# One beat's delay for the weight preparation that falls on the first beat of a softmax chunk

## The chip, the cores and the metric

The kernel runs on one core of a Trainium2 chip. The metric is the time of one execution in microseconds (us), as the median of several runs. The engines are TensorE (PE in the profile, with its weight loads as PEld), VectorE (DVE), ScalarE (ACT), GpSimd (POOL) and SyncE (SP, which here only issues DMAs). They run side by side, each in its own program order, and wait for each other by semaphores.

## The reference

Attention with normalised queries and keys over 8 batches of 12 heads, 448 rows and 64 columns, and behind it a feed-forward block with a maximum of three products. All is float32.

```
q_n, k_n = rmsnorm(q, g_q), rmsnorm(k, g_k)
scores = scale * q_n @ k_n^T
attn = softmax(scores)                       # row maximum subtracted
attn_out = attn @ v                          # (8, 12, 448, 64)
x = attn_out as (3584, 768)
h = maximum(maximum(x @ w1, x @ w2), x @ w3) # (3584, 768)
out = h @ w_out                              # (3584, 768)
```

## The kernel before

Two heads make a pair; there are 48 pairs `g`, six to a batch. The 448 rows of a pair are worked in four chunks `c` of 112 rows. The program is a list of beats: `beat(g, i)` with `i` from 0 to 11, three beats to a chunk, so the beat's number is `12 g + i` and the first beat of a chunk is one whose number is divisible by 3. Every engine's order is the order in which the beats issue its instructions; nothing reorders them afterwards.

For a chunk numbered `k = 4 g + c` the steps are:

- first beat: `row_max` (L562, DVE) finds the negated maxima of the two heads' scores; `softmax` scales them (`nm`, L570, ACT) and takes two exponentials with their row sums (L579, ACT); then `lower_weights` of the chunk before (L665, DVE, two instructions) runs, the last reader of that chunk's scores.
- second beat: `upper_weights` takes the reciprocal of the sums (`rs`, L648 and L652, DVE) and writes the softmax weights as float16 (`pp`, L655, ACT, two instructions).
- third beat: PE does the scores of the next chunk (L553). The scores live in two PSUM buffers in turn, so they need the buffer that `lower_weights` of the chunk before has read.

Each number is kept as an upper float16 part and a lower one (the rest), and three products of parts make one product. The first six pairs (`PLAIN = 6`) are done otherwise, in plain float32.

Beside that, `thirds` issues in each beat two or three steps of the feed-forward block of an earlier batch (L732 layer 1, L796 layer 2), which fill PE. Further work is put off with `later(beats, work, last)` into the table `due`; `tick`, the last call of a beat, issues what is due at the current number `clock[0]`, first the works without `last`, then those with it.

The weights are prepared in 24 blocks: 18 of w1, w2 and w3, then 6 of w_out. In the program's view they come as pairs of 32-bit words. `prep_block(n)` is called at the first beat after `4 n` for n up to 18 and at the first after `72 + 8 (n - 18)` beyond. It has these steps:

- `rebias` (L188, ACT), at once;
- `decode` in three stages 2, 3 and 4 beats later (L196, L200, L205, DVE);
- for a block of w_out `row_largest` (L170, DVE) 5 beats later, and `load_raw` (L223 or L228, SP), the load of block n + 2 into the one of two buffers that the decode has emptied.

After the third block of a column group, `bound_in` takes its maximum and turns it into a scale, and then each of the three blocks is split: `upper` (L268, L269, ACT) and two beats later `lower` (L272, POOL). After the last block `bound_out` does the same for w_out, where `upper` (L307, ACT) and `lower` (L312, DVE) of the six blocks follow at one beat's distance. The unsplit block lies one slot on from where its split parts go, so `upper` of a block overwrites what `lower` of the block before reads.

Of the kernel before, what the change touches and what calls it, by code (L numbers as in the profile page):

```python
# [35 lines left out]
PLAIN = 6  # L36
# [3 lines left out]
def qknorm_attention_maxout_ffn_kernel(  # L40
# [69 lines left out]
    due = {}  # L110
    clock = [0]

    def later(beats, work, last=False):

        due.setdefault(clock[0] + beats, ([], []))[last].append(work)

    def tick():
        while clock[0] in due:
            for works in due.pop(clock[0]):
                for work in works:  # L120
                    work()
        clock[0] += 1


    ident = const.tile([P, P], F32, name="ident")
# [51 lines left out]
    o_row = const.tile([P, NFT], F32, name="o_row")  # L177
# [56 lines left out]
    def prep_block(n):  # L234
        kind, ft, j = blocks[n]
        raw = raws[n]
        f = plain(w_sb, n) if kind == "in" else plain(wo_sb, ft)
        rebias(raw)

        for stage in range(3):  # L240
            later(2 + stage, lambda stage=stage: decode(raw, f, stage), True)
        if kind == "out":
            later(5, lambda: row_largest(o_row[:, ft:ft + 1], f), True)
        later(5, load_raw)
        if j == NJ - 1:
            later(5, lambda: bound_in(ft), True)
        elif kind == "out" and ft == NFT - 1:
            later(6, bound_out)

    def bound_in(ft):  # L250
        most = sb.tile([P, 1], F32, name="most", bufs=2)
        n = ft * NJ + 1
        row_largest(
            most, w_sb[:, n:n + NJ].rearrange("p n a f -> p (n a f)").bitcast(F32)
        )

        def scale(bound):
            top, up = w_most[:, ft:ft + 1], w_up[:, ft:ft + 1]
            nc.vector.tensor_scalar(
                out=top, in0=bound, scalar1=LEAST, scalar2=None, op0=ALU.max  # L260
            )
            nc.vector.reciprocal(up, top)
            nc.vector.tensor_scalar(
                out=up, in0=up, scalar1=UP, scalar2=None, op0=ALU.mult
            )

            def upper(n, f):
                nc.scalar.activation(f, f, AF.Copy, scale=up)  # L268
                nc.scalar.copy(w_sb[:, n, 0], f)  # L269

            def lower(n, f):
                nc.gpsimd.tensor_tensor(  # L272
                    out=w_sb[:, n, 1], in0=f, in1=w_sb[:, n, 0], op=ALU.subtract
                )

            for j in range(NJ):
                n = ft * NJ + j
                f = plain(w_sb, n)
                later(2 + 4 * j, lambda n=n, f=f: upper(n, f), True)
                later(4 + 4 * j, lambda n=n, f=f: lower(n, f), True)  # L280

        largest(most, scale, (3, 2, 4, 1))


    def bound_out():
        by = const.tile([P, NFT], F32, name="o_block")
        most = const.tile([P, 1], F32, name="o_most")
        nc.vector.tensor_tensor(out=by, in0=o_row, in1=w_most, op=ALU.mult)
        nc.vector.tensor_reduce(most, by, axis=AX, op=ALU.max)

        def scale(bound):
            nc.vector.tensor_scalar(
                out=o_up, in0=bound, scalar1=LEAST ** 2, scalar2=None, op0=ALU.max
            )
            nc.vector.reciprocal(most, o_up)
            nc.vector.tensor_scalar(
                out=by, in0=w_most, scalar1=most, scalar2=2.0 * UP,
                op0=ALU.mult, op1=ALU.mult,
            )

            nc.vector.tensor_scalar(
                out=o_up, in0=o_up, scalar1=DM / 2.0 / (2.0 * UP), scalar2=None,
                op0=ALU.mult,
            )

            def upper(ft):
                nc.scalar.activation(  # L307
                    wo_sb[:, ft, 0], plain(wo_sb, ft), AF.Copy, scale=by[:, ft:ft + 1]
                )

            def lower(ft):
                nc.vector.scalar_tensor_tensor(  # L312
                    out=wo_sb[:, ft, 1], in0=plain(wo_sb, ft), scalar=by[:, ft:ft + 1],
                    in1=wo_sb[:, ft, 0], op0=ALU.mult, op1=ALU.subtract,
                )
                split.append(ft)

            for ft in range(NFT):
                later(ft + 1, lambda ft=ft: upper(ft), True)
                later(ft + 2, lambda ft=ft: lower(ft), True)  # L320

        largest(most, scale, (1, 2, 2, 2))


# [600 lines left out]
    def beat(g, i):  # L925
        w, n = g - 1, g + 2
        c, part = divmod(i, 3)
        k = 4 * g + c
        early = k + 1 <= 4 * PLAIN
        if part == 0:  # L930
            if g < G:
                if k > 4 * PLAIN:
                    row_max(g, c)
                softmax(g, c)
            if early:
                scores(*divmod(k + 1, 4))
            if 0 < k <= 4 * PLAIN:
                turn_plain(*divmod(k - 1, 4))
            elif 0 < k <= 4 * G:
                lower_weights(*divmod(k - 1, 4))  # L940
        if part == 1:
            if 0 < k <= 4 * PLAIN:
                keep_turned(*divmod(k - 1, 4))
            if PLAIN <= g < G:
                upper_weights(g, c)
        if part == 2:
            if early:
                row_max(*divmod(k + 1, 4))
            elif k + 1 < 4 * G:
                scores(*divmod(k + 1, 4))  # L950
        if 0 <= w < PLAIN:
            if i == 1:
                guard_sums(w)
            if i == 2:
                inverse_sums(w)
            if i == 5:
                spread_sums(w)
            if i == 6:
                keep_sums(w)
            if i == (8 if w < PLAIN else 9):  # L960
                scale_plain(w)
        if w >= 0 and i == (4 if w < PLAIN else 7):
            add_values(w)
        thirds(THIRDS[i] + (len(queue) > 1 and i % 6 == 4))
        if w >= 0 and i == (9 if w < PLAIN else 10):
            finish(w, x_of[w // NP])
        if w >= 0 and g % NP == 0 and i == (6 if w < PLAIN else 10):
            queue.append(ffn(w // NP, x_of[w // NP]))

        if g + 1 < G:  # L970
            if g + 1 < PLAIN:
                if i in (1, 4):
                    turn_whole(g + 1, "kq"[i // 4])
                if i in (2, 5):
                    keep_whole(g + 1, "kq"[i // 5])
            else:
                if i in (0, 1):
                    upper_rows(g + 1, "kq"[i])
                if i in (2, 3):
                    lower_rows(g + 1, "kq"[i - 2])  # L980
                if i in (4, 5):
                    turn_rows(g + 1, "kq"[i - 4])

        if n < G:
            if i in (0, 3):
                squares(n, "kq"[i // 3])
            if i in (2, 5):
                sum_squares(n, "kq"[i // 3])
            if i in (5, 7):
                inv_rms(n, "kq"[i // 7])  # L990
            if i == 8:
                scale_k(n)
            if i == 9:
                scale_q(n)

        if g == 0 and i < 7:
            load_v(i)
            later(3, lambda: largest_v(i))
        if 0 < g < G - 6 and i == 5:
            load_v(g + 6)  # L1000
            later(4, lambda: largest_v(g + 6))
        if g == 0 and i == 9:
            bound_v(0)
        if g > 1 and g % NP == 0 and g < G and i == 1:
            bound_v(g // NP)
        if PLAIN <= g < G and i == 9:
            scale_v(g)
        if PLAIN <= g < G and i == 11:
            upper_v(g)
        if PLAIN <= w and i == 0:  # L1010
            lower_v(w)

        if g + 3 < G:
            if i == 0:
                load_k(g + 3)
            if i == 1:
                load_q(g + 3)
        if i == 2 and w >= PLAIN:
            turn_weights(w, 3)
        if PLAIN <= g < G and i in (5, 8, 11):  # L1020
            turn_weights(g, i // 3 - 1)
        n_in = min(decoded[0], NFT * NJ)
        due_at = BLOCK_BEATS[0] * n_in + BLOCK_BEATS[1] * (decoded[0] - n_in)
        if decoded[0] < len(blocks) and clock[0] > due_at:
            later(0, lambda n=decoded[0]: prep_block(n), True)
            decoded[0] += 1
        tick()

# [40 lines left out]
```

## Time and profile before

| | |
|---|---|
| median of 3 runs | 1101.73 us |
| lowest, highest | 1098.24, 1102.97 us |
| the profiled execution | 1103.44 us |
| its span, first to last instruction | 1101.6 us |
| mean granted TensorE clock | 0.957 |
| busy: PE, DVE, ACT, POOL | 1018.6, 757.8, 772.1, 702.4 us |

In the rows of the profile the first two numbers of an instruction are its start in us from the beginning of the span and its duration; then come engine, line, operation, the tile written and those read, their shapes, and how many were merged (x2). Square brackets hold the idle time of the engine just before, and whose work ended it. A row of waits names who waited, for whom, the total, the number of times and the longest. A row of groups gives the busy time and the mean duration in ns. Granted clock 1.00 is full speed.

### The profile page before, as it was taken

How to read it: one execution, taken by the hardware profiler on the slowest of the kernel's cores; microseconds unless marked ns; L12 is line 12 of the kernel's file. 1: busy time of each engine (PE TensorE's matmuls, PEld its weight loads, DVE VectorE, ACT ScalarE, POOL GpSimd, SP SyncE). 2: the span in 40 equal slices, each digit the busy share in tenths (PEclk: the TensorE clock that was granted, in tenths of full speed). 3: DMA queues.
4: the chain of work that ended last, by engine and by line, in shares of the span. 5: the costliest groups of instructions: out<-in, count | busy, mean ns of one | idle time of the engine just before them, and what ended most of it. 6: DMA issues, size and time to landing. Idle time of an engine off the chain costs nothing. (4 is left out here: it accounts for less than half of the span.)

```text
span 1101.6 us, 18390 instructions
## 1 busy us (share of the span) xinstructions
PE 1018.6 (92%) x6168; PEld 501.9 (46%) x6168; DVE 757.8 (69%) x1390; ACT 772.1 (70%) x1767; POOL 702.4 (64%) x805
## 2 busy tenths in 40 slices
PE   4678768988999999999999999999999999999998
PEld 2334333434444455444544454444444454445555
DVE  3899988888667676677677776777677766762210
ACT  4599887767868678687877777778777787773001
POOL 5477988856767767678677686776867677610000
PEclk9687868998989999999999999999999999999999
DMA  5554466856787679877888789787877798563002
GB/s 149 165 164 152 129 180 137 179 115 125 151 166 149 134 151 172 160 148 133 176 155 149 136 169 175 141 151 150 170 146 143 145 166 153 106 106 73 1 1 58
DMA packets 426654, 152.29 MB, mean 138 GB/s; under 512 B 372928, under 2 KB 422336, under 8 KB 426560
## 3 DMA queue, kind: packets, MB, share of 16 engines
q1 hardware_dynamic: 425888, 150.75, 66.8%
q8 instruction: 48, 0.79, 0.3%
q10 hardware_dynamic: 672, 0.38, 0.1%
q14 instruction: 46, 0.38, 0.1%
HBM read 51.97 MB, written 11.01 MB: 57 GB/s over the span
## 5 line engine op out<-in xcount | busy, mean ns | idle before, releaser
L732 PE MATMUL acc<-xt,w_sb 128*128 128x448 f16 x2592 | 520.6, 356 | 0.6 <-ACT m L742 0.6
L732 PEld LDWEIGHTS <-w_sb 128*128 128x128 f16 x2592 | 245.1, 99 | 262.9 <-issue 53.1
L562 DVE TENSOR_REDUCE sc<-sc 112x2 f32<-112x896 f32 x192 | 209.7, 1092 | 47.8 <-PE sc L553 46.6
L579 ACT ACTIVATE sc<-sc,nm,down 112x448 f32<-112x448 f32 x336 | 234.2, 697 | 11.2
L655 ACT ACTIVATE pp<-sc,rs 112x448 f16<-112x448 f32 x336 | 194.8, 632 | 48.5 <-ACT sc L579 40.4
L665 DVE SCALAR_TENSOR_TENSOR pp<-sc,rs,pp 112x448 f16<-112x448 f32 x336 | 212.9, 675 | 3.4 <-ACT pp L655 2.9
L387 POOL TENSOR_TENSOR ri<-ri,half_neg 128x7 f32<-128x7 f32 x96 | 154.2, 1606 | 8.0
L553 PE MATMUL sc<-kt,qt 64*112 64x448 f16 x1008 | 133.7, 371 | 27.1 <-DVE pp L665 23.6
L570 ACT ACTIVATE nm<-sc,down 112x2 f32<-112x2 f32 x192 | 50.7, 264 | 149.5 <-DVE sc L562 148.2
L796 PE MATMUL acc<-wo_sb,ht 128*128 128x384 f16 x864 | 151.4, 330 | 1.4 <-DVE ht L756 0.8
L761 POOL COPY hx<-ht 128x128 f16<-128x128 f16 x48 | 15.5, 323 | 197.7 <-DVE ht L756 191.7
L796 PEld LDWEIGHTS <-ht 128*128 128x128 f16 x864 | 82.0, 99 | 67.5 <-issue 14.5
L703 PE MATMUL av<-pt,vp 128*64 128x448 f16 x1008 | 108.3, 356 | 0.0
L553 PEld LDWEIGHTS <-qt 64*112 64x112 f16 x1008 | 55.0, 128 | 96.9 <-issue 56.4
L648 DVE TENSOR_SCALAR rs<-sc 112x2 f32<-112x2 f32 x168 | 26.6, 158 | 94.7 <-ACT sc L579 94.7
L440 POOL TENSOR_TENSOR kp<-kn,kp 128x512 f16<-128x512 f32 x42 | 50.0, 1190 | 58.9 <-ACT kp L434 58.9
L703 PEld LDWEIGHTS <-vp 128*64 128x64 f16 x1008 | 49.6, 108 | 56.0 <-issue 30.4
L718 DVE SCALAR_TENSOR_TENSOR xt<-av,xt 128x448 f16<-128x448 f32 x42 | 26.2, 625 | 71.1 <-ACT xt L717 71.1
L372 DVE TENSOR_REDUCE ss<-sq 128x7 f32<-128x448 f32 x96 | 60.9, 635 | 10.6 <-ACT sq L363 6.6
L531 POOL TENSOR_TENSOR vp<-vr,vp 128x448 f16<-128x448 f32 x42 | 43.8, 1044 | 32.2 <-ACT vp L525 32.1
L440 POOL TENSOR_TENSOR qp<-qn,qp 112x512 f16<-112x512 f32 x42 | 49.3, 1173 | 21.0 <-ACT qp L434 20.8
L517 POOL TENSOR_SCALAR vr<-vr,v_up 128x448 f32<-128x448 f32 x42 | 60.7, 1446 | 0.0
(112 smaller groups left out, 1203.1 us busy)
## 6 DMA issues: line engine op xcount, KB each, us to landing
raw<-in_moe_w_dram SPq DMA_DIRECT2D x18, 768.0 KB, 4.4
qr<-in_q_dram SPq DMA_DIRECT2D x48, 224.0 KB, 3.0
vr<-in_v_dram SPq DMA_DIRECT2D x96, 96.0 KB, 2.5
kr<-in_k_dram SPq DMA_DIRECT2D x95, 96.0 KB, 3.0
raw<-in_moe_w_out_dram SPq DMA_DIRECT2D x6, 768.0 KB, 5.1
pt<-pp SPq DMA_TRANSPOSE x168, 4.1
out_dram<-osb SPq DMA_DIRECT2D x8, 336.0 KB, 3.2
out_dram<-osb SPq DMA_DIRECT2D x8, 288.0 KB, 3.7
```

What stands on the lines that cost most here:

```text
L372: nc.vector.tensor_reduce(sums[g % 2][:sq.shape[0], KQ[what]], sq, axis=AX, op=ALU.add)
L387: nc.gpsimd.tensor_tensor(out=ri, in0=ri, in1=half_neg[:, at], op=ALU.pow)
L440: nc.gpsimd.tensor_tensor(out=parts[:, 1], in0=n, in1=parts[:, 0], op=ALU.subtract)
L517: nc.gpsimd.tensor_scalar(out=vr, in0=vr, scalar1=v_up[:, g // NP:g // NP + 1], scalar2=None, op0=ALU.mult,)
L553: nc.tensor.matmul(sc[:QP, h, :S], qt[rows, qp, c], kt[rows, kp, KEYS[h]], start=n == 0, stop=n == len(TERMS) - 1,)
L562: nc.vector.tensor_reduce(sc[:QP, 0, S + 8:S + 10], sc[:QP, :, :S], axis=AX, op=ALU.max, negate=True)
L579: nc.scalar.activation(to, sc[:QP, h, :S], AF.Exp, bias=nm[:, h:h + 1], scale=down[:QP], accum_out=total,)
L655: nc.scalar.activation(pp[:, 0, h], sc[:QP, h, :S], AF.Copy, scale=rs[:, h:h + 1])
L665: nc.vector.scalar_tensor_tensor(out=pp[:, 1, h], in0=sc[:QP, h, :S], scalar=rs[:, h:h + 1], in1=pp[:, 0, h], op0=ALU.mult, op1=ALU.subtract,)
L703: nc.tensor.matmul(av[half, :S], vp[rows, group, vpart], pt[rows, 7 * wp + group], start=u == 0 and n == 0, stop=u == 3 and n == len(TERMS ...
L732: nc.tensor.matmul(acc[:, :S], wt[:, wp, c], xs[c][:, xp], start=(c == 0 and n == 0), stop=(c == NCT - 1 and n == 2),)
L796: nc.tensor.matmul(acc[:, :HW], lhs, wo_sb[:, f, wp, half * HW:(half + 1) * HW], start=(f == 0 and n == 0), stop=(f == NFT - 1 and n == 2),)
```

## The change

`later` gets a fourth argument that names an engine. When `tick` comes to a work with such a name in a beat whose number is divisible by 3 and at least `12 * PLAIN = 72`, which is the first beat of a chunk from the seventh pair on, it does not issue the work but puts it at the head of the `last` list of the next beat. Named are the decode stages, the maxima and the loads, `prep_block` itself and the split of the weights, but for `lower` of w1 to w3 on POOL. `load_raw` and `bound_out` also move from the first list to the `last` one. `prep_block` counts its later steps from the beat in which it is issued, so a block whose preparation is put off has all its steps one beat later. No instruction is added, removed or altered.

```
-    def later(beats, work, last=False):
+    def later(beats, work, last=False, on=None):
-        due.setdefault(clock[0] + beats, ([], []))[last].append(work)
+        due.setdefault(clock[0] + beats, ([], []))[last].append((work, on))
+
+    def busy(on):
+        return on is not None and clock[0] % 3 == 0 and clock[0] >= 12 * PLAIN

     def tick():
+        put_off = []
         while clock[0] in due:
             for works in due.pop(clock[0]):
-                for work in works:
-                    work()
+                for work, on in works:
+                    if busy(on):
+                        put_off.append((work, on))
+                    else:
+                        work()
         clock[0] += 1
+        if put_off:
+            due.setdefault(clock[0], ([], []))[1][:0] = put_off
...
         for stage in range(3):
-            later(2 + stage, lambda stage=stage: decode(raw, f, stage), True)
+            later(2 + stage, lambda stage=stage: decode(raw, f, stage), True, "dve")
         if kind == "out":
-            later(5, lambda: row_largest(o_row[:, ft:ft + 1], f), True)
-        later(5, load_raw)
+            later(5, lambda: row_largest(o_row[:, ft:ft + 1], f), True, "dve")
+        later(5, load_raw, True, "dve")
         if j == NJ - 1:
-            later(5, lambda: bound_in(ft), True)
+            later(5, lambda: bound_in(ft), True, "dve")
         elif kind == "out" and ft == NFT - 1:
-            later(6, bound_out)
+            later(6, bound_out, True, "dve")
...
-                later(2 + 4 * j, lambda n=n, f=f: upper(n, f), True)
+                later(2 + 4 * j, lambda n=n, f=f: upper(n, f), True, "act")
                 later(4 + 4 * j, lambda n=n, f=f: lower(n, f), True)
...
-                later(ft + 1, lambda ft=ft: upper(ft), True)
-                later(ft + 2, lambda ft=ft: lower(ft), True)
+                later(ft + 1, lambda ft=ft: upper(ft), True, "act")
+                later(ft + 2, lambda ft=ft: lower(ft), True, "dve")
...
-            later(0, lambda n=decoded[0]: prep_block(n), True)
+            later(0, lambda n=decoded[0]: prep_block(n), True, "act")
```

## The prediction

> **What bounds the kernel now.** I read the page, then the stretches in time, then the waits and instructions of the one stretch that the change reaches.
>
> ```profile
> span 1101.6 us, 18390 instructions
> ...
> PE 1018.6 (92%) x6168; PEld 501.9 (46%) x6168; DVE 757.8 (69%) x1390; ACT 772.1 (70%) x1767; POOL 702.4 (64%) x805
> ...
> raw<-in_moe_w_out_dram SPq DMA_DIRECT2D x6, 768.0 KB, 5.1
> ```
>
> ```profile
> 140.00:285.00 145.00, 122.52 (x683) 58.05 (x684) 122.23 (x213) 110.65 (x238) 111.01 (x113) 0.87 0.67 145
> 285.00:1000.00 715.00, 703.15 (x4441) 342.34 (x4439) 508.44 (x1001) 543.21 (x1273) 494.29 (x590) 1.00 0.78 149
> ```
>
> The columns of the second view are the stretch, then busy time of PE, weight loads, DVE, ACT, POOL, then granted clock. TensorE bounds the whole. From 285 us on it is busy 98% (703.15 of 715) at clock 1.00, so only a gap or a slow clock before that can be gained or lost. The moved work is all issued between beats 72 and 133 (a beat is `12 g + i`), about 145 to 273 us by their rows below. There PE is busy 84%, as is DVE, and the clock is 0.87: neither engine bounds it alone, but the chain between them.
>
> ```profile
> ACT nm L570 <- DVE sc L562: 21.5, 13, 3.0
> PE sc L553 <- DVE pp L665: 16.3, 8, 3.9
> ...
> DVE rs L648 <- ACT sc L579: 9.5, 13, 1.4
> ```
>
> These are waits in the same 145 us (total, times, longest). PE's scores of chunk k+2 wait for `lower_weights(k)` (L665) on DVE, which frees the score buffer: 16.3 us over 8 waits, the most that better DVE order could give back besides the clock. L665 stands on DVE behind the `row_max` (L562) of chunk k+1. The last row is what matters here: after `lower_weights` of the chunk before, DVE mostly waits for ScalarE's exponentials before `rs` (L648). That gap is in the chunk's first beat, where the moved DVE work stood. After `rs` DVE goes on to the next `row_max` mostly without a gap.
>
> ```profile
> 175.32 2.44 PE L732 MATMUL acc<-xt,w_sb 128*128 128x448 f16 x12
> ...
> 182.08 1.37 PE L553 MATMUL sc<-kt,qt 64*112 64x448 f16 x6 [2.41 <-DVE pp L665]
> 183.38 4.63 PE L732 MATMUL acc<-xt,w_sb 128*128 128x448 f16 x12
> ...
> 211.19 0.78 PE L553 MATMUL sc<-kt,qt 64*112 64x448 f16 x6 [1.02 <-DVE pp L665]
> ...
> 222.48 0.78 PE L553 MATMUL sc<-kt,qt 64*112 64x448 f16 x6 [1.66 <-DVE pp L665]
> ...
> 229.26 1.37 PE L553 MATMUL sc<-kt,qt 64*112 64x448 f16 x6 [2.49 <-DVE pp L665]
> ...
> 270.64 1.37 PE L553 MATMUL sc<-kt,qt 64*112 64x448 f16 x6 [3.22 <-DVE pp L665]
> ```
>
> A PE wait has a second price. After 1.66 us idle the scores took 0.78, after 2.41 and more 1.37, and 12 matmuls then took 4.63 where 2.44 is usual: a slow restart costs (1.37 - 0.78) + (4.63 - 2.44) = 2.8 us.
>
> **The change part by part.** A block n from 18 on is prepared at beat 73 + 8(n - 18), decoded 2, 3 and 4 beats later, its maximum and the next load 5 later. Work tagged `dve` or `act` and due at a beat divisible by 3, from 72, goes one later: stage 1 of block 17 (72), stage 0 of 18 (75), maximum of 18, load, `upper` of 13 (78), rebias of 19 (81, and with it all its stages, of which those that land on 84 and 87 move twice), `upper` of 16 (90), stage 2 of 20 (93), stage 0 of 21 (99), its maximum and load (102), rebias of 22 (105, its stages likewise), stage 2 of 23 (117), and of w_out `upper` 2 and `lower` 1 (129), `upper` 5 and `lower` 4 (132). No instruction is added or removed.
>
> ```profile
> 145.18 1.35 DVE L200 SCALAR_TENSOR_TENSOR w_sb<-raw,w_sb 128x768 uint32<-128x768 uint32 x1
> 147.93 0.16 DVE L648 TENSOR_SCALAR rs<-sc 112x2 f32<-112x2 f32 x1 [1.41 <-ACT sc L579]
> ...
> 148.26 2.68 DVE L205 SCALAR_TENSOR_TENSOR w_sb<-raw,w_sb 128x768 uint32<-128x768 uint32 x1
> ...
> 156.11 0.55 DVE L196 TENSOR_SCALAR wo_sb<-raw 128x768 uint32<-128x768 uint32 x1
> 156.92 0.16 DVE L648 TENSOR_SCALAR rs<-sc 112x2 f32<-112x2 f32 x1 [0.27 <-ACT sc L579]
> ...
> 161.96 0.94 DVE L170 TENSOR_REDUCE o_row<-wo_sb 128x1 f32<-128x768 f32 x1
> ...
> 166.04 1.27 DVE L665 SCALAR_TENSOR_TENSOR pp<-sc,rs,pp 112x448 f16<-112x448 f32 x2 [1.17 <-ACT pp L655]
> ...
> 173.44 2.43 DVE L200 SCALAR_TENSOR_TENSOR wo_sb<-raw,wo_sb 128x768 uint32<-128x768 uint32 x1
> 175.80 0.15 DVE L648 TENSOR_SCALAR rs<-sc 112x2 f32<-112x2 f32 x1
> ...
> 176.06 1.64 DVE L205 SCALAR_TENSOR_TENSOR wo_sb<-raw,wo_sb 128x768 uint32<-128x768 uint32 x1
> ...
> 191.27 1.10 DVE L562 TENSOR_REDUCE sc<-sc 112x2 f32<-112x896 f32 x1 [1.56 <-PE sc L553]
> ...
> 241.07 0.94 DVE L205 SCALAR_TENSOR_TENSOR wo_sb<-raw,wo_sb 128x768 uint32<-128x768 uint32 x1
> ```
>
> ```profile
> L200 DVE SCALAR_TENSOR_TENSOR wo_sb<-raw,wo_sb 128x768 uint32<-128x768 uint32 x6 | 8.1, 1355 | 0.1
> ...
> L196 DVE TENSOR_SCALAR wo_sb<-raw 128x768 uint32<-128x768 uint32 x6 | 6.7, 1110 | 0.1
> L205 DVE SCALAR_TENSOR_TENSOR wo_sb<-raw,wo_sb 128x768 uint32<-128x768 uint32 x6 | 6.4, 1063 | 0.0
> ```
>
> The same decode instruction takes 0.55 or up to 2.43: some are stretched. Taking 0.55 (L196 at 156.11) and 0.94 (L205 at 241.07, and the same for L200) as unstretched, the three rows of w_out hold 21.2 - 6 x (0.55 + 0.94 + 0.94) = 6.6 us of stretch. POOL is busy 111 of the 145 us; I take the stretch to be a wait for it. The Trainium skill, "SBUF — State Buffer", section "Who interferes with whom", says that VectorE and GpSimd share one port pair under an exclusive lock, held for a whole instruction, which a VectorE instruction with two SBUF inputs or in a two-port mode needs. The rows agree in kind; by that rule each moved decode draws its stretch anew, so the sum keeps its mean and the range grows.
>
> *Beats 72 and 75.* DVE waits for ACT behind both anyway (1.41, 0.27), so they were free; behind `rs` they delay the next `row_max` by 0.94 + 0.55 = **+1.5**. Ends: +0.5 if only stage 0 shows; +3.2 if stage 1 pushes L205 behind another POOL instruction (2.68 - 0.94 more).
>
> *Beat 78.* The maximum adds 0.94 ahead of the next `row_max`, but L665 there waits 1.17 for ACT's weights, which stood behind `upper` and now do not: **0** (-0.2 to +0.9, if that wait stays).
>
> *Beats 81 to 88.* Here the old order did hurt:
>
> ```profile
> 173.96 0.13 ACT L579 ACTIVATION_READ_ACCUMULATOR sc<-sc,nm,down 112x1 f32 x1
> ```
>
> The exponentials are done at 174.09, `rs` runs at 175.80, held 1.7 by a stretched stage 1. Behind `rs` go then stages 0 and 1 (0.55 + 0.94), and the maximum (0.94) leaves for beat 88: -1.7 + 0.55 = -1.15 at best, -1.8 if L205 too loses its 0.7 of stretch, 0 if both stretch again; I take **-0.8**, nearer the best. The PE wait of 2.41 at 182.08 then falls to about 1.6, where 1.66 stayed warm. That would save 2.8, yet DVE is the later one soon after: its wait for PE at 191.27 is 1.56, less the 0.94 now put in at beat 88, so some 0.7 counts, at an even chance: **-0.35**. Without that 1.56 the 0.94 itself would show.
>
> ```profile
> 204.37 0.55 DVE L196 TENSOR_SCALAR wo_sb<-raw 128x768 uint32<-128x768 uint32 x1
> 205.53 0.16 DVE L648 TENSOR_SCALAR rs<-sc 112x2 f32<-112x2 f32 x1 [0.62 <-ACT sc L579]
> ...
> 211.05 0.94 DVE L170 TENSOR_REDUCE o_row<-wo_sb 128x1 f32<-128x768 f32 x1
> ...
> 218.38 1.86 DVE L196 TENSOR_SCALAR wo_sb<-raw 128x768 uint32<-128x768 uint32 x1
> ...
> 229.93 0.16 DVE L648 TENSOR_SCALAR rs<-sc 112x2 f32<-112x2 f32 x1 [0.73 <-ACT sc L579]
> ```
>
> *Beat 93* only trades places with `rs`: **0** (-0.25 to +0.5). *Beat 99:* a free slot (0.62 left idle) is given up: **+0.55**, and PE's wait at 211.19 grows from 1.02, still warm. *Beats 102 to 110:* the maximum goes behind `rs`, +0.6 (0.94 less what the next L665 waits anyway, estimated 0.3); the stretched stage 0 leaves its place before a `row_max`, -(1.86 - 0.55) = -1.3; at beat 109 two stages fill what one had, and the idle slot of 0.73 (as at 229.93) is back, +0.4. Sum **-0.3** (-1.3 to +0.7). *Beats 111 and 117:* +0.94 hidden by PE's values and layer-1 matmuls between, and `rs` 0.94 sooner for stage 2 later: **0** (-0.5 to +0.9).
>
> ```profile
> L307 ACT ACTIVATE wo_sb<-wo_sb,o_block x6: 932/935/942, 258.5 to 271.7; 128x768 f16<-128x768 f32 x6
> L312 DVE SCALAR_TENSOR_TENSOR wo_sb<-wo_sb,o_block x6: 1008/1019/1180, 259.4 to 272.7; 128x768 f16<-128x768 f32 x6
> ```
>
> ```profile
> 265.08 1.02 DVE L312 SCALAR_TENSOR_TENSOR wo_sb<-wo_sb,o_block 128x768 f16<-128x768 f32 x1 [0.73 <-ACT wo_sb L307]
> ...
> 272.69 1.18 DVE L312 SCALAR_TENSOR_TENSOR wo_sb<-wo_sb,o_block 128x768 f16<-128x768 f32 x1 [0.62 <-ACT wo_sb L307]
> ```
>
> *Beats 129 and 132.* w_out is split in place, each block into the slot that the next `upper` overwrites, so `lower` n and `upper` n+1 take turns on DVE and ACT. Now `lower` 1, `upper` 2, `lower` 2, `upper` 3 are issued in one beat: DVE does 1.02, waits 0.94 for ACT, does 1.02; and again at 133. Behind them stand the `row_max` of the next chunks. One such turn (0.94) at the scores of 270.64, slow already, and about 0.6 more at those after: **+1.6** (0.6 if DVE's present waits of 0.73 and 0.62 cover one; 2.5 if stretched).
>
> *ACT's rebias and `upper` elsewhere:* 0; the softmax weights come sooner, but of the rows above L665 waited for them only at 166.04. If ACT were behind instead, the moved work would delay `nm` (L570), which has 21.5 us of waits here to cover it. *SP's loads:* one or two beats later, still behind the decode that frees their buffer, 5.1 us to land, while the block is first read some ten beats later: 0; the transposes behind them on SP wait no longer than for that decode.
>
> Sum: 1.5 + 0 - 0.8 - 0.35 + 0 + 0.55 - 0.3 + 0 + 1.6 = **+2.2 us**, all ahead of the stretch that PE fills, so it reaches the end. The profiled execution took 1103.4 (span 1101.6 and 1.8 around it), 1.7 above the median; 1105.6 on it is **1103.9** on the median of 1101.73.
>
> **The rivals.** (a) *Faster: the slow restarts go.* The stalls at 182.08 and 229.26 end under some 2 us and PE stays warm; it decides if both fall and DVE keeps up. -2 x 2.8, and the full -1.8 of beats 81 to 88, against the other +3.4 (2.2 + 0.8 + 0.35, rounded): -4.0, **1097.7**. For it: 2.41 is near 1.66; against: DVE is 84% busy and 229.26's stall does not shrink in my sum.
> (b) *Slower: stretch or restarts come on top.* The 1.02 and 1.66 waits, or that before 156.92, pass the threshold, 2.8 each, and the upper ends at beats 72 and 129 (+1.7, +0.9): +2.2 + 2.8 + 2.6 = +7.6, **1109.3**. It decides from 1 us of growth at one of them. The Trainium skill, "TensorE: Matmul & The Clock Gate", Part 1, gives about 3.4 us of idleness for half clock, on a free-running window; by that, the phase and not the length of a 2.4 us stall would decide, and restarts could come and go at any of them. The slow restarts after 2.41 and 2.49 show that less than 3.4 is enough here.
> (c) *Nothing.* The moved work finds other gaps: **1101.7**. For it: some 20 instructions of about 1 us in 1100; against: the two places without cover, 72 and 129.
>
> **How the numbers follow.** Forecast 0.58, (a) 0.13, (b) 0.18, (c) 0.11. The ends of the terms add to -2.9 and +9, hardly all at once; the range goes from (a)'s side, 1098.4, to (b)'s, 1109.2, leaving out half of (a) and half of (b). About 0.5% (5.5 us) is what a measurement of this kernel can tell from no change. Faster by more (under 1096.2) is the far part of (a), 0.06; slower by more (over 1107.2) most of (b), 0.15; the rest 0.79.
>
> **What would show it.** Right: `rs` near 148 waits about 2.7 instead of 1.41, the idle ahead of `rs` up to 285 us grows past 9.5; L307 and L312 near 264 wait for each other about 1 us; the scores after them wait over 4 us; from 285 on nothing differs. Wrong: PE's wait for L665 falls well under 16.3, the clock of the stretch rises over 0.87, or time moves after 285 us.

## The result, and the profile after

The change makes the kernel slower. Beside each other on one chip, nine runs each:

| | before | after |
|---|---|---|
| median | 1098.75 us | 1106.35 us |
| lowest, highest | 1096.30, 1102.97 us | 1103.48, 1107.59 us |
| ratio after to before | | 1.0058 (1.0040 to 1.0076) |

By the ratio the change costs +6.4 us (+4.4 to +8.3); the two medians stand 7.6 apart. The forecast was +2.2 on a median of three runs that was 1101.73. The 1103.9 that it gave is nearer to the measured time than the +2.2 is to the difference, because those three runs stood higher than the nine do.

First the page of the profile after, then its stretches in time.

```profile
span 1104.8 us, 18388 instructions
...
PE 1018.2 (92%) x6168; PEld 502.0 (45%) x6168; DVE 757.2 (69%) x1390; ACT 773.1 (70%) x1767; POOL 702.9 (64%) x805
```

```profile
140.00:285.00 145.00, 117.97 (x644) 55.97 (x643) 119.05 (x206) 106.95 (x227) 106.10 (x105) 0.86 0.66 140
285.00:1000.00 715.00, 703.88 (x4462) 342.69 (x4460) 508.86 (x1003) 545.53 (x1278) 497.56 (x595) 1.00 0.78 150
```

Every engine does the same work over the whole span (PE 1018.2 against 1018.6, DVE 757.2 against 757.8). From 285 us on the stretch is as it was, PE busy 703.88 against 703.15. Between 140 and 285 us every engine did less than before in the same time: PE 117.97 against 122.52, DVE 119.05 against 122.23. So nothing was added. The two spans lie only 3.2 us apart because the profiled execution before, with 1103.44, was one of the longer ones. The chain through that stretch got longer, as the prediction placed it.

These are the waits between 140 and 290 us (total, times, longest).

```profile
PE sc L563 <- DVE pp L675: 21.1, 9, 4.1
...
DVE rs L658 <- ACT sc L589: 16.3, 21, 2.7
```

The second of them before, over the same 150 us (the prediction's 9.5 is over 145):

```profile
DVE rs L648 <- ACT sc L579: 9.7, 14, 1.4
```

(Lines after are ten higher: L658 is `rs`, L589 the exponentials, L572 `row_max`, L675 `lower_weights`, L563 the scores, L206, L210 and L215 the decode stages, L180 a maximum, L322 `lower` of w_out.) DVE's wait ahead of `rs` grew from 9.7 to 16.3: the slots that the moved work used to fill now stand empty. PE's wait for `lower_weights` grew from 16.3 to 21.1: that work now stands ahead of the next `row_max`, and what follows from `row_max` comes later. ScalarE's wait for `row_max` (`nm`) grew with it, from 22.9 to 28.0 over the same 150 us.

Beats 72 and 75 on DVE in after, and POOL in the same microseconds:

```profile
147.16 0.16 DVE L658 TENSOR_SCALAR rs<-sc 112x2 f32<-112x2 f32 x1 [2.72 <-ACT sc L589]
...
147.50 3.15 DVE L210 SCALAR_TENSOR_TENSOR w_sb<-raw,w_sb 128x768 uint32<-128x768 uint32 x1
150.69 1.80 DVE L215 SCALAR_TENSOR_TENSOR w_sb<-raw,w_sb 128x768 uint32<-128x768 uint32 x1
...
155.47 1.08 DVE L572 TENSOR_REDUCE sc<-sc 112x2 f32<-112x896 f32 x1
...
158.47 0.16 DVE L658 TENSOR_SCALAR rs<-sc 112x2 f32<-112x2 f32 x1 [0.74 <-ACT sc L589]
...
159.00 0.54 DVE L206 TENSOR_SCALAR wo_sb<-raw 128x768 uint32<-128x768 uint32 x1
```

```profile
147.09 1.64 POOL L282 TENSOR_TENSOR w_sb<-w_sb 128x768 f16<-128x768 f32 x1
148.69 1.15 POOL L450 TENSOR_TENSOR kp<-kn,kp 128x512 f16<-128x512 f32 x1
150.18 1.49 POOL L450 TENSOR_TENSOR qp<-qn,qp 112x512 f16<-112x512 f32 x1 [0.34 <-ACT qp L444]
```

`rs` waits 2.72 where it waited 1.41, as announced (about 2.7). Behind it stage 1 took 3.15 and stage 2 1.80, where 0.94 is unstretched and where before stage 2 alone stood, with 2.68. Both end equally long after POOL came free: the first 0.81 after 148.69 + 1.15 = 149.84, the second 0.82 after 150.18 + 1.49 = 151.67. What the upper end of the term named came about: stage 1 pushed stage 2 behind another POOL instruction. From `rs` to the next `row_max` it is now 155.47 - 147.16 = 8.31; before it was 6.00, from 147.93 to this row:

```profile
153.93 1.08 DVE L562 TENSOR_REDUCE sc<-sc 112x2 f32<-112x896 f32 x1
```

To see where it adds up I take the start of PE's scores of four chunks, in each trace counted from the first `rs` behind 145 us (chunk 24). The table gives the us from each mark to the next. Rows from the third on are of kernels with single parts of the change, told of below.

| kernel | `rs` 24 to scores 27 | to 34 | to 44 | to 48 |
|---|---|---|---|---|
| before | 14.16 | 42.42 | 58.22 | 25.47 |
| after | **17.07** | **41.61** | 58.88 | **28.08** |
| no work moved, lists only | 14.39 | 39.83 | 58.48 | 25.21 |
| beats 72, 75 alone | **16.72** | 40.04 | 58.52 | 25.21 |
| beats 78 to 117 alone | 14.40 | **41.60** | 58.82 | 25.39 |
| beats 78 to 87 alone | 14.01 | **41.68** | 58.50 | 25.40 |
| beat 93 alone | 14.38 | 39.86 | 58.51 | 25.22 |
| beats 99 to 117 alone | 14.39 | 39.91 | 58.85 | 25.22 |
| beats 129, 132 alone | 14.07 | 39.82 | 58.48 | **28.08** |

Three columns are clear: against the rows that leave the beats in question as they were, the first has +2.3 to +3.1, the second +1.6 to +1.9, the last +2.6 to +2.9. In the third the kernels that put off beats 99 to 117 have some 0.3 more. The trace before stands apart in the second column: of the traces in the table it alone holds an `rs` back by 1.7 us at chunk 28 (175.80, in the prediction). So the row of lists only, in which no work is moved, is the better measure for that column.

### The profile page after: what moved, and what is told of

Same layout as the page of the kernel before. It is cut to its first block, busy times and chain, and to the rows that moved or that the text cites. A ratio compares the mean times of both kernels' runs of the same rounds, so it can differ in the third digit from the quotient of the medians.

```text
span 1104.8 us, 18388 instructions
## 1 busy us (share of the span) xinstructions
PE 1018.2 (92%) x6168; PEld 502.0 (45%) x6168; DVE 757.2 (69%) x1390; ACT 773.1 (70%) x1767; POOL 702.9 (64%) x805
## 5 line engine op out<-in xcount | busy, mean ns | idle before, releaser
L589 ACT ACTIVATE sc<-sc,nm,down 112x448 f32<-112x448 f32 x336 | 234.4, 698 | 11.2
L572 DVE TENSOR_REDUCE sc<-sc 112x2 f32<-112x896 f32 x192 | 209.7, 1092 | 45.7 <-PE sc L563 44.5
L675 DVE SCALAR_TENSOR_TENSOR pp<-sc,rs,pp 112x448 f16<-112x448 f32 x336 | 212.9, 675 | 1.9 <-ACT pp L665 1.5
L563 PE MATMUL sc<-kt,qt 64*112 64x448 f16 x1008 | 133.4, 370 | 31.4 <-DVE pp L675 28.1
L563 PEld LDWEIGHTS <-qt 64*112 64x112 f16 x1008 | 55.0, 127 | 101.3 <-issue 60.6
L658 DVE TENSOR_SCALAR rs<-sc 112x2 f32<-112x2 f32 x168 | 26.7, 159 | 101.9 <-ACT sc L589 101.9
```

Of the source, the lines that this page charges most:

```text
L563: nc.tensor.matmul(sc[:QP, h, :S], qt[rows, qp, c], kt[rows, kp, KEYS[h]], start=n == 0, stop=n == len(TERMS) - 1,)
L572: nc.vector.tensor_reduce(sc[:QP, 0, S + 8:S + 10], sc[:QP, :, :S], axis=AX, op=ALU.max, negate=True)
L589: nc.scalar.activation(to, sc[:QP, h, :S], AF.Exp, bias=nm[:, h:h + 1], scale=down[:QP], accum_out=total,)
L675: nc.vector.scalar_tensor_tensor(out=pp[:, 1, h], in0=sc[:QP, h, :S], scalar=rs[:, h:h + 1], in1=pp[:, 0, h], op0=ALU.mult, op1=ALU.subtract,)
```

## The experiments

Each was timed in alternation with the kernel before (five rounds unless told), and differences are against it.

**The change in two halves and its tail.** In the changed kernel only the condition in `busy` is narrowed:

```
-        return on is not None and clock[0] % 3 == 0 and clock[0] >= 12 * PLAIN
+        return on is not None and clock[0] in (72, 75)                        # first
+        return on is not None and clock[0] % 3 == 0 and 78 <= clock[0] <= 117 # second
+        return on is not None and clock[0] in (129, 132)                      # third
```

First, beats 72 and 75:

> Only the two decode stages due at beats 72 and 75 are put off a beat, all other weight work stands where it stood before (the loads and bound_out stay in the last list, as in the changed kernel). Theory (the first beat of a chunk has a free slot on VectorE ahead of rs, and work put behind rs costs its own length, plus the stretch by GpSimd that it meets there): +2.9 us on the kernel before, 1.5 of it slot and 1.4 stretch, the scores of chunk 27 2.9 us later against the rs near 148 us. Rival (the loss of the changed kernel comes from ScalarE's moved work or from the loads): within 0.5 us of the kernel before.

Measured 1101.0 against 1098.52: ratio 1.0023 (1.0012 to 1.0033), +2.5 us. The theory holds, and in the trace the scores of chunk 27 come 2.6 later than before (16.72 against 14.16); the rival of at most 0.5 falls.

Second, beats 78 to 117:

> Only the works due at beats 78 to 117 are put off, ScalarE's rebias and upper and SyncE's loads among them; 72, 75, 129 and 132 stand as before. Theory: about 0 (-1.0 to +1.5 us), since the slots given up and the held rs set free cancel. Rival (every work moved out of a first beat costs about its 0.8 us, nine of them): +6 us or more. Second rival (the moved ScalarE work is the cause): the whole +6.4 us is here.

Measured 1101.55: 1.0021 (1.0011 to 1.0031), +2.3 us. This was a miss: the theory had about nothing here, as the prediction did. The rival's +6 is excluded too.

Third, beats 129 and 132:

> Only the splitting of w_out due at beats 129 and 132 is put off. Theory (lower 1, upper 2, lower 2, upper 3 now take turns inside one beat, with row_max of the next chunk behind them): +2.6 us, a wait of VectorE for L317 of over 1 us near 268 us, and over 4 us of idle TensorE ahead of the scores of chunk 45. Rival (the splitting is hidden, since layer 2 reads the blocks later): 0, no longer wait of TensorE there.

Measured 1102.19: 1.0028 (1.0015 to 1.0041), +3.1 us, as expected; in its trace PE waits 4.11 us ahead of the scores of chunk 45. The three come to 7.9, the whole to 6.4 (4.4 to 8.3): the parts add up within what they are known to.

**No work moved, lists only.** `busy` returns False, so that only the move of the loads and of `bound_out` between the two lists is left.

```
-        return on is not None and clock[0] % 3 == 0 and clock[0] >= 12 * PLAIN
+        return False
```

> The changed kernel with nothing put off: what is left of the change is that load_raw and bound_out stand in the last list of their beat. Theory: 0 (within 1 us), the loads land long before they are read. Rival (part of the loss in each of the three part kernels, whose losses add to 7.9 where the whole has 6 to 7.6, is this reordering, which all three hold): +0.5 to +1.5 us.

Measured 1098.57 against 1098.46: 1.0005 (0.9995 to 1.0015), so -0.5 to +1.6 us. No cost of the order of the lists shows, but this interval alone does not exclude the rival's +0.5 to +1.5. The three kernels below that come to -0.1, +0.3 and 0.0 hold the same order, which speaks against it.

**Only ScalarE's work of beats 78 to 117.**

```
-        return on is not None and clock[0] % 3 == 0 and clock[0] >= 12 * PLAIN
+        return on == "act" and clock[0] % 3 == 0 and 78 <= clock[0] <= 117
```

> Of beats 78 to 117 only ScalarE's works are put off: upper of blocks 13 and 16 and the preparation of blocks 19 and 22, whose decodes come a beat later for it but are not put off themselves. Theory (the +2.3 us of beats 78 to 117 is VectorE's work behind rs, above all stage 2 of block 20 at beat 94, stretched there, and the maximum of block 19 at beat 88): 0 (-1 to +0.7). Rival (ScalarE's work and what follows from the later preparation carries it): +2.

Measured 1099.87: 0.9999 (0.9986 to 1.0012), at most +1.3 us, though the two medians stand 1.4 apart. The rival's +2 is excluded. ScalarE's part, and the decodes that come a beat later with it, cost nothing that shows, and so the +2.3 is at least in the main what VectorE's own work adds by being put off.

**The middle in three.** The same line, with `clock[0] == 93`, with `78 <= clock[0] <= 87 and clock[0] % 3 == 0`, and with `99 <= clock[0] <= 117 and clock[0] % 3 == 0`.

> Only the work of beat 93 (stage 2 of block 20) goes a beat later. In the run that put off beats 78 to 117, PE's scores of chunk 33 began 12.15 us after those of chunk 31, against 10.85 and 10.84 where beat 93 was as before: stage 2 was stretched behind rs. Theory (the stretch behind rs at beat 93 is half of that run's +2.3): +1.0 to +1.5. Rival (the prediction's price: stage 2 and rs only trade places): within 0.5 of before.

> Only the work of beats 78 to 87 goes a beat later (the maximum of block 18 and its load, rebias of 19 with its stages and maximum). Theory (no rs is held up in most runs, so there is nothing to save, and the stages and the maximum behind rs delay the next maxima): +0.5 to +1.3, from the scores of chunk 31, which began 25.1 us after those of chunk 27 in the run that put off beats 78 to 117 and 24.4 and 24.2 in two runs that left these beats alone. Rival (the prediction's: a held rs is freed, -0.8 and a part of a restart): -0.5 to -1.8.

> Only the work of beats 99 to 117 goes a beat later. Theory: 0 (-0.4 to +0.5), since PE's scores of chunk 44 began 51.55 us after those of chunk 35 with these beats put off and 51.8 where they were not, and with the two runs above it makes up the +2.3 of beats 78 to 117. Rival (these beats carry a good part of the +2.3, by POOL's stretch drawn anew): +1 or more.

Measured against 1098.81: beat 93 alone 1099.39, 1.0003 (0.9992 to 1.0014), +0.3; beats 78 to 87 1101.16, 1.0022 (1.0013 to 1.0031), +2.4; beats 99 to 117 1098.86, 1.0000 (0.9990 to 1.0009). My theory had shared the +2.3 between beat 93 and beats 78 to 87. It belongs to beats 78 to 87, above the theory's upper end of 1.3, though its sign is right; for beat 93 the rival, which was the prediction's price, is favoured, and +1.0 to +1.5 lies at the far end of the interval. For beats 99 to 117 the theory of 0 holds. The theory for the first two had read the scores of chunk 31 alone. With beats 78 to 87 put off those of chunk 33 come 11.72 behind them, against 10.84 with beats 129 and 132 put off, and this second part of the loss I had put down to beat 93.

DVE in the kernel with beats 78 to 87 put off:

```profile
172.40 0.16 DVE L658 TENSOR_SCALAR rs<-sc 112x2 f32<-112x2 f32 x1 [1.62 <-ACT sc L589]
...
172.67 1.08 DVE L206 TENSOR_SCALAR wo_sb<-raw 128x768 uint32<-128x768 uint32 x1
173.78 1.80 DVE L210 SCALAR_TENSOR_TENSOR wo_sb<-raw,wo_sb 128x768 uint32<-128x768 uint32 x1
...
176.57 0.94 DVE L215 SCALAR_TENSOR_TENSOR wo_sb<-raw,wo_sb 128x768 uint32<-128x768 uint32 x1
177.43 1.08 DVE L572 TENSOR_REDUCE sc<-sc 112x2 f32<-112x896 f32 x1
...
180.43 0.16 DVE L658 TENSOR_SCALAR rs<-sc 112x2 f32<-112x2 f32 x1 [0.74 <-ACT sc L589]
...
180.71 0.93 DVE L180 TENSOR_REDUCE o_row<-wo_sb 128x1 f32<-128x768 f32 x1
...
182.68 1.09 DVE L572 TENSOR_REDUCE sc<-sc 112x2 f32<-112x896 f32 x1
```

and in the one with beats 129 and 132 put off, which here is as before, first at beats 84 to 87 and then at beat 93:

```profile
171.91 0.95 DVE L210 SCALAR_TENSOR_TENSOR wo_sb<-raw,wo_sb 128x768 uint32<-128x768 uint32 x1
173.79 0.16 DVE L658 TENSOR_SCALAR rs<-sc 112x2 f32<-112x2 f32 x1 [0.94 <-ACT sc L589]
...
174.07 2.09 DVE L215 SCALAR_TENSOR_TENSOR wo_sb<-raw,wo_sb 128x768 uint32<-128x768 uint32 x1
...
177.14 0.94 DVE L180 TENSOR_REDUCE o_row<-wo_sb 128x1 f32<-128x768 f32 x1
178.00 1.08 DVE L572 TENSOR_REDUCE sc<-sc 112x2 f32<-112x896 f32 x1
...
181.00 0.16 DVE L658 TENSOR_SCALAR rs<-sc 112x2 f32<-112x2 f32 x1 [0.74 <-ACT sc L589]
...
182.39 1.09 DVE L572 TENSOR_REDUCE sc<-sc 112x2 f32<-112x896 f32 x1
...
190.56 1.35 DVE L215 SCALAR_TENSOR_TENSOR wo_sb<-raw,wo_sb 128x768 uint32<-128x768 uint32 x1
191.84 0.14 DVE L658 TENSOR_SCALAR rs<-sc 112x2 f32<-112x2 f32 x1
...
194.43 1.09 DVE L572 TENSOR_REDUCE sc<-sc 112x2 f32<-112x896 f32 x1
...
197.94 0.16 DVE L658 TENSOR_SCALAR rs<-sc 112x2 f32<-112x2 f32 x1 [1.24 <-ACT sc L589]
```

With the beats as before, stage 1 (0.95) fits into the slot ahead of `rs` and `rs` still waits 0.94 for ScalarE. Put off, the slot is empty (1.62), and all three stages stand between `rs` and `row_max` (1.08, 1.80, 0.94) where a stretched stage 2 (2.09) and the maximum (0.94) stood: it is 177.43 - 172.40 = 5.03 against 178.00 - 173.79 = 4.21. In the next chunk the maximum stands behind `rs`: 182.68 - 180.43 = 2.25 against 182.39 - 181.00 = 1.39. Together that is +1.7, and the table has as much at the scores of chunk 34 (41.68 against 39.82), so nothing gives it back; timed were +2.4.

Beat 93 in the kernel with that beat alone put off, whose rows up to there stand within 0.1 us of those above, shows how a move can be free:

```profile
190.96 0.16 DVE L658 TENSOR_SCALAR rs<-sc 112x2 f32<-112x2 f32 x1 [0.21 <-ACT sc L589]
...
191.24 1.78 DVE L215 SCALAR_TENSOR_TENSOR wo_sb<-raw,wo_sb 128x768 uint32<-128x768 uint32 x1
...
194.99 1.09 DVE L572 TENSOR_REDUCE sc<-sc 112x2 f32<-112x896 f32 x1
...
197.99 0.16 DVE L658 TENSOR_SCALAR rs<-sc 112x2 f32<-112x2 f32 x1 [0.74 <-ACT sc L589]
```

Stage 2 is stretched to 1.78 behind `rs`, and `rs` to `row_max` takes 4.03 against 2.59. But that `row_max` comes 0.56 later, not 1.44, since `rs` itself ran 0.88 sooner, and the next `rs` waits 0.74 where 1.24 was idle: 197.99 against 197.94, so it is all recovered. The scores of chunk 33 still came 0.56 later (197.31 against 196.75), those of chunk 34 no more (201.63 against 201.58).

**More work in either place.** In the kernel before, 120 extra maxima over 128x768 in pairs 12 to 41, ahead of `rs` in the first beat of each chunk, or behind it in the second (one round, two executions of each). The one other line added declares the tile `extra`.

```
         ... first beat, ahead of upper_weights     # one kernel
+            if 12 <= g < 42:
+                row_largest(extra, wo_sb[:, 0]...)
         ... second beat, behind rs                  # the other, the same lines
```

> The kernel before with one extra maximum over 128x768 (0.94 us on VectorE, 0.86 from start to start, its result unused) for each of the 120 chunks of pairs 12 to 41, at the end of the first beat, ahead of rs. Theory (VectorE waits 0.56 us on average ahead of rs, 0.74 in a usual chunk): most of it is free: +5 us (0 to +20) for 113 us of added work. Rival (only VectorE's total counts): the same as the kernel with the extra work in the second beat, within 5 us.

> The same 120 extra maxima, but in the second beat, behind rs. Theory: the slot ahead of rs stays empty, and 0.86 us a chunk comes on top of VectorE's chain: +40 us (+15 to +75), at the least 15 us more than with the work ahead of rs. Rival (only the total counts): no difference from that kernel over 5 us.

Measured +18.4 (1.0168, 1.0147 to 1.0189) and +27.1 (1.0247, 1.0228 to 1.0267). The same 120 instructions cost 8.7 us less ahead of `rs`, so the rival falls; both sizes were off, the first expected too low and the second too high, and the difference is smaller than the theory's 15. Waits ahead of `rs` between 285 and 940 us, 77.5 in the kernel before, in the kernel with the work behind `rs`:

```profile
DVE rs L649 <- ACT sc L580: 72.2, 111, 1.1
```

and the group of `rs` with the work ahead of it, over the same stretch:

```profile
L649 DVE TENSOR_SCALAR rs<-sc 112x2 f32<-112x2 f32 x130 | 19.7, 152 | 10.5 <-ACT sc L580 10.1
```

Behind `rs`, the slots stay empty (72.2). Ahead of it, the maxima fill all but 10.1 of them. A slot holds only some 72.2 / 111 = 0.65 us and a maximum takes 0.94, so ahead of `rs` was not free either. Nor did the work behind `rs` cost its full length, 120 x 0.86 = 103 us from start to start: it filled other waits of VectorE that come later. The wait for ScalarE ahead of the instruction that writes `xt` fell from 53.7 us before to 26.1 (52.5 with the work ahead of `rs`), and the wait of `row_max` for PE's scores from 40.2 to 4.6 (27.3).

**The other way: fill the slot.** In the kernel before, two sums of squares per pair go from the third beat of a chunk to the first beat of the next:

```
-            if i in (2, 5):
-                sum_squares(n, "kq"[i // 3])
+            if i in ((2, 5) if g < PLAIN else (3, 6)):
+                sum_squares(n, "kq"[i // 5 if g < PLAIN else i // 6])
```

> The kernel before, with the two sums of squares of a pair (0.64 us each on VectorE) issued a beat later from the seventh pair on: from the third beat of a chunk, ahead of the next row_max, into the first beat of the next chunk, ahead of rs. Theory (the slot there is free): VectorE's waits for ScalarE ahead of rs (94.7 us in all before) fall by some 40 us, and in the stretch up to 285 us each move saves up to 0.55 us where VectorE is late: -3 us (-5.6 to 0); behind 285 us TensorE is full and nothing is gained. Rival (the slot's position does not matter, only VectorE's total): 0. Second rival (the later sums delay GpSimd's scaling and with it keys and queries): slower.

Measured 1096.81 against 1098.52: 0.9983 (0.9973 to 0.9993), -1.9 us (-3.0 to -0.8). It is faster than both kernels, and DVE's waits for ScalarE ahead of `rs` fall from 94.7 to 50.0 us over the whole span, as expected; both rivals fall. And with the maxima of blocks 19 and 22 moved from the third beat to the next first one as well:

```
-            later(5, lambda: row_largest(o_row[:, ft:ft + 1], f), True)
+            later(6 if clock[0] % 3 == 0 else 5, lambda: row_largest(o_row[:, ft:ft + 1], f), True)
```

> The kernel before with the sums of squares in the first beat of a chunk (the faster version) and, beside it, the maxima of blocks 19 and 22 moved from the third beat of a chunk (86 and 110) to the first of the next (87 and 111), where DVE waits for ScalarE anyway. Theory (work ahead of rs is free up to the wait, work elsewhere delays the next row_max): 0.3 to 1.5 faster than the faster version, so -2.2 to -3.4 against before. Rival (PE's values and layer steps cover the third beat): as the faster version, -1.9.

Measured 1094.72 against 1098.81: 0.9961 (0.9946 to 0.9976), -4.3 us (-5.9 to -2.6). It is the fastest of all, and the sign of the step follows the rule; its size over the former, 2.4, is more than the 0.3 to 1.5 expected. The two were not timed beside each other and their intervals overlap at the ends, so the step by itself is likely and not shown. Its waits between 140 and 290 us:

```profile
PE sc L553 <- DVE pp L665: 12.7, 8, 3.5
...
DVE rs L648 <- ACT sc L579: 5.8, 9, 1.5
```

Both rows moved opposite to the change: 12.7 against 16.3 before and 21.1 after, 5.8 against 9.7 and 16.3.

It is not free of collisions. On DVE, ahead of `rs` of chunk 28:

```profile
171.29 4.14 DVE L200 SCALAR_TENSOR_TENSOR wo_sb<-raw,wo_sb 128x768 uint32<-128x768 uint32 x1
175.35 0.15 DVE L648 TENSOR_SCALAR rs<-sc 112x2 f32<-112x2 f32 x1
```

Stage 1 is stretched to 4.14 and holds `rs` for 3.0 us behind the exponentials (done at 172.35). So this version has something left there; I did not try it.

## Why the prediction was right or wrong

The place was right, and in the main the mechanism: only 145 to 285 us matters, nothing is added, free slots ahead of `rs` are given up, `row_max` comes later, PE waits longer for `lower_weights`. The sign of the forecast was right. That the time of 1103.9 lies no more than 2.5 from the measured 1106.35 is in part luck, since its base stood 3 us higher than the median of nine. Counted from that base the range reached from -3.3 to +7.5, and +6.4 lies near its upper end. The sum was a third of the measured difference, by three terms:

| term of the sum | forecast | timed alone |
|---|---|---|
| beats 72 and 75 | +1.5 | +2.5 (1.3 to 3.6) |
| beat 78, beats 81 to 88 | 0 - 0.8 - 0.35 | +2.4 (1.4 to 3.4) |
| beat 93 | 0 | +0.3 (-0.9 to 1.5) |
| beats 99, 102 to 110, 111, 117 | +0.55 - 0.3 + 0 | 0.0 (-1.1 to 1.0) |
| beats 129 and 132 | +1.6 | +3.1 (1.6 to 4.5) |
| ScalarE's work, beats 78 to 117 | 0 | -0.1 (-1.5 to 1.3) |

*Beats 72 and 75* were mis-sized: the mechanism that the upper end named occurred. Of the 2.9 in the trace (17.07 against 14.16), 2.3 come from the two stages that now stand behind the first `rs` (8.31 against 6.00), where the sum had 0.94.

*Beats 81 to 88* is the step that failed. It credited the change with freeing an `rs` that had been held 1.7 us by a stage 1 stretched to 2.43. In five other traces with these beats as before, `rs` was held 0.2 us or less (unstretched at 171.91 in the rows above, with 0.94 of wait to spare). Only the two kernels with the sums of squares moved showed such a hold again (3.0 us). The cover for the maximum at beat 88, DVE's wait of 1.56 at 191.27, was as little to be relied on: it followed that run's slow restart at 182.08, and the other traces have no such wait there. Without the two accidents the same working gives a loss: three stages between `rs` and `row_max` where one and the maximum were, and 0.93 of maximum behind the next `rs`, +1.7 in the rows above. "Without that 1.56 the 0.94 itself would show" stood there; that was the case.

*Beats 129 and 132*: the turns were foreseen, and their price was too low. The rows of after:

```profile
265.63 1.33 DVE L322 SCALAR_TENSOR_TENSOR wo_sb<-wo_sb,o_block 128x768 f16<-128x768 f32 x1
268.25 1.02 DVE L322 SCALAR_TENSOR_TENSOR wo_sb<-wo_sb,o_block 128x768 f16<-128x768 f32 x1 [1.29 <-ACT wo_sb L317]
...
277.19 1.54 DVE L322 SCALAR_TENSOR_TENSOR wo_sb<-wo_sb,o_block 128x768 f16<-128x768 f32 x1 [1.40 <-ACT wo_sb L317]
```

The waits are 1.29 and 1.40, where I took 0.94, the bare duration of `upper`, for one and 0.6 for the other; and two of the blocks were stretched, to 1.33 and 1.54. PE's scores behind them waited over 4 us, as announced (4.12 below).

*The restarts.* I read a threshold between 1.66 and 2.41 us of idleness from one trace, and a price of 2.8 us. Neither holds. Scores with their waits in after, and for one the 12 matmuls behind:

```profile
157.78 1.37 PE L563 MATMUL sc<-kt,qt 64*112 64x448 f16 x6 [3.73 <-DVE pp L675]
...
230.93 0.91 PE L563 MATMUL sc<-kt,qt 64*112 64x448 f16 x6 [3.52 <-DVE pp L675]
231.77 3.95 PE L742 MATMUL acc<-xt,w_sb 128*128 128x448 f16 x12
...
273.53 1.37 PE L563 MATMUL sc<-kt,qt 64*112 64x448 f16 x6 [4.12 <-DVE pp L675]
```

After 3.52 the scores took only 0.91, but the 12 behind them 3.95 where 2.44 is usual: the slow stretch came a little later. At chunk 30 after waited 2.49 and was slow (1.37, and 3.41 for the 12 behind); with beats 78 to 117 alone put off, PE waited 2.91 there and was at full speed (0.78 and 2.44). So no threshold on the length alone exists in this range. Yet both reach the scores of chunk 34 after 41.6 us, so that restart cost nothing that lasted. Half of 0.7 for a stall that falls under a threshold was credit for nothing.

Rival (b) came nearest with its +7.6: what its two upper ends named did come, at +2.5 and +3.1, and one stall that it named, at the scores of chunk 26 (1.41 before), did become a slow restart (3.73, 1.37, first row). But the restarts as a whole did not get more frequent: between 140 and 285 us five scores took 1.37 in either trace, at a granted clock of 0.86 against 0.87. So what it put on top for them is not shown as a cause; the term that it lacked was beats 81 to 88.

## What to carry to other kernels

Where an in-order engine always waits for the same partner at one place of a loop, side work ahead of that place fills the wait. The same work one place later leaves that wait empty and costs what no later wait of the engine covers: 27.1 us instead of 18.4 for 120 maxima, and +6.4 for this change, while the filled slot gave -1.9. So put it there, no longer than the wait, and check that two moved pieces do not come to stand in one place. Price such a move from the rows of more than one run where that is to be had, and do not credit a change with removing a stretch, a held instruction or a slow restart that one trace shows once. Where a timed part comes out otherwise than its terms say, split it further before explaining it: the +2.3 of beats 78 to 117 was one group, beats 78 to 87.

## What the runs showed of the hardware

How long PE was idle does not by itself set the speed of its restart. The same wait in three kernels, first with beat 93 put off, then with no work moved, then with beats 78 to 87 put off, each with the 12 matmuls behind it:

```profile
226.40 0.78 PE L563 MATMUL sc<-kt,qt 64*112 64x448 f16 x6 [2.49 <-DVE pp L675]
227.10 2.44 PE L742 MATMUL acc<-xt,w_sb 128*128 128x448 f16 x12
```

```profile
226.81 0.78 PE L563 MATMUL sc<-kt,qt 64*112 64x448 f16 x6 [2.49 <-DVE pp L675]
227.51 4.13 PE L742 MATMUL acc<-xt,w_sb 128*128 128x448 f16 x12
```

```profile
226.65 1.37 PE L563 MATMUL sc<-kt,qt 64*112 64x448 f16 x6 [2.49 <-DVE pp L675]
227.95 3.31 PE L742 MATMUL acc<-xt,w_sb 128*128 128x448 f16 x12
```

At the same scores, after the same 2.49 us and with the same work around, one runs at full speed throughout, one slows down only behind the scores, and one runs the scores themselves at about half. The Trainium skill, "TensorE: Matmul & The Clock Gate", Part 1, has PE's activity judged over a free-running window of about 3.4 us; by that it is the phase that decides, and these rows agree in kind, but show slow restarts after waits shorter than the window. Whether such draws also move whole runs is not shown. The profiled execution before, with slow restarts after 2.41, 2.49 and 3.22 us, took 1103.44 where the median of nine is 1098.75, but it also held an `rs` back by 1.7 us, and the restart of after at chunk 30 had left nothing by chunk 34.

A VectorE instruction that is stretched beside GpSimd can sit through more than the GpSimd instruction in flight: the 3.15 us of stage 1 at 147.50 span the end of one and all of the next, and end 0.81 after GpSimd came free at 149.84. The 4.14 us at 171.29 in the kernel with the sums and the maxima moved span the end of one and all of the next two, and end 0.82 after GpSimd came free at 173.46 + 1.15 = 174.61.
